# A list scheduler that lets the successive instructions of one engine overlap, and plans the exponential and the maximum of the softmax with other durations

## The chip, the core and the metric

The kernel runs on one core of a Trainium2 chip. The core has a matrix engine (TensorE, PE in the profile), a vector engine (VectorE, DVE), a scalar engine (ScalarE, ACT), a general engine (GpSimd, POOL) and a queue engine that here only issues DMAs (SyncE, SP). Each engine takes its own instructions strictly in the order in which the program lists them, and waits at semaphores for the others. The metric is the device time of one execution in microseconds, lower is better. Three executions of the kernel before took 2626.95, 2629.58 and 2632.05 us; the median is 2629.58 us.

## The reference

One block of a transformer over 2048 tokens of width 448: a layer norm, then attention with 16 heads of width 28 and a mixture of 8 experts, both added to the input. All 8 experts take part in every token (K = E = 8), so the mixture is dense and its gates are a plain softmax.

```python
xn = layernorm(x)
# attention, 16 heads of 28
q, k, v = split(xn @ wqkv)
p = softmax(q @ k.T * 28 ** -0.5)
out = x + (p @ v) @ wo
# mixture, for e in range(8):
out += gate[e] * (silu(xn @ w1[e]) @ w2[e])      # 448 -> 1792 -> 448
```

Inputs and output are float32.

## The kernel before

Every float32 factor of a large product is scaled by a power of two and split into two float16 halves, high and low, and the product is made of three float16 products. That multiplies PE's work, and it gives the other engines the work of splitting.

**Stages.** `phase0` loads and normalizes the input, makes queries, keys and values, writes them to DRAM, and prepares the first weights. Then two streams of work are mixed until the end.

- **The mixture** (`moe`): 24 groups of 4 or 5 blocks of 128 hidden columns. For each group the weights are loaded (`load_group`), their largest magnitudes are found and sent through DRAM so that all partitions have them (`group_scales`, `scales`: the DMA `mxs<-mxr` writes, the DMA `scmg<-mxs` reads, and DVE's chain from L358 to L368 makes the scale `scog` of it), and they are split on ACT (L463, L464, L481, L482) and POOL (L468, L485). The hidden products are L898 (with a small tail, L906), their activation goes ACT L940 (tanh), DVE L943, ACT L946 (high half) and POOL L947 (low half), the second products are L962, and DVE adds them up in L974.
- **Attention** (`attention`): 256 tiles, one for each head and 128 queries. A tile has two **scores** of 128 x 1024, each of two matmuls (L1058, 512 score pairs in all). DVE takes the row maximum of a score (L1062), ACT takes the exponential (L1076), ACT and DVE split the result (L1084 high, L1087 low), the halves are transposed by DMA (L1101), and PE multiplies them by the values (L1135, L1142). Only one score pair can be in PSUM at a time: it has banks 0 and 1, and the next pair waits until the exponential has read the last one. The six other banks hold all other products.

**What sets the order.** The program's order is not written by hand. Each piece of work is a `Job` with an engine, a planned duration `ns`, a due time `v` and its dependencies. `Plan.run` plays the plan through on a clock of its own: whenever an engine is free in the plan, it takes the ready job with the smallest due time whose buffers and banks are to be had, emits its instructions, and marks the engine busy for `ns`. What depends on the job becomes ready `ns` plus a lag later (180 ns behind PE, 60 ns behind ACT and DVE, 90 ns behind POOL). DMAs have a planned transfer time and a planned landing time. So planned durations decide the order on every engine, and on the chip nothing but this order is left of them.

```python
free[e] = t + j.ns
end = t + j.ns + j.lag
if j.size:
    dma = max(dma, t + 1000) + j.size
    end = dma + (LAND if j.v > 1 else 1000)
```

A maximum is planned at 1330 ns and an exponential at 1205 ns before the change.

Of the kernel before, what the change touches and what calls it, by code (L numbers as in the profile page):

```python
# [35 lines left out]
SEL = 512.0  # L36
NB, TL, TH = 4, 1, 4
RW1, RW2, RH, RP = 9, 9, 7, 1
QK_SCALE = DH ** -0.5
XS = 8.0  # L40
HUGE = 3.0e38
# [17 lines left out]
class Plan:  # L59
# [2 lines left out]


    LAG = {"PE": 180, "ACT": 60, "DVE": 60, "POOL": 90, "SP": 0}

    def __init__(self):
        self.jobs, self.wrote, self.read, self.order = [], {}, {}, {}
# [37 lines left out]
    def run(self, pools, banks):  # L105
# [3 lines left out]
        free = dict.fromkeys(self.LAG, 0)  # L109
        live, given = {}, {}  # L110
        events, t, dma, left = [], 0, 0, len(self.jobs)
# [42 lines left out]
        while left:  # L154
            moved = True
            while moved:
                moved = False
                for e in ready:
# [14 lines left out]
                        b.real = pools.get(b.pool).tile(b.shape, b.dtype, tag=b.tag, name=b.name, bufs=b.bufs)  # L173
                    j.fn()
                    left -= 1
                    free[e] = t + j.ns
                    end = t + j.ns + j.lag
                    if j.size:
                        dma = max(dma, t + 1000) + j.size
# [10 lines left out]
            t = events[0][0]  # L190
# [74 lines left out]
def block_kernel(ctx, tc, x, wqkv, wo, w_gate, w1, w2, out):  # L265
# [741 lines left out]
    def attention(at):  # L1007
# [39 lines left out]
        def score(i, j, v):  # L1047
            h, t = TILES[i]
            if i % NB == 0 and j == 0:
                mx[i] = buf("ap", [P, NB, 2], F32, f"mx{i}", tag="mx", bufs=3)  # L1050
            q0 = t % TPC * P
            sc[i, j] = b = ps_s(f"ps{i}_{j}")
            q, k, m, n = Q[h, t // TPC], K[h, j], mx[i // NB * NB], i % NB

            def product():
                for a in range(2):
                    cs = slice(a * C, (a + 1) * C)
                    nc.tensor.matmul(b()[:, cs], q()[:, q0 : q0 + P], k()[:, cs], start=True, stop=True)  # L1058

            add("PE", 2 * Z_NS, product, v, r=[(q, g) for g in range(4)] + [(k, g) for g in range(4)], w=[b])  # L1060
            def top():
                nc.vector.tensor_tensor_reduce(  # L1062
                    b(), b(), zero.to_broadcast([P, 2 * C]), cneg, HUGE,
                    op0=ALU.add, op1=ALU.min, accum_out=m()[:, n, j : j + 1],
                )

            add("DVE", 1330, top, v, r=["cexp"], w=[b, (m, n, j)])

        def expo(i, j, v):

            if j == 0:
                PR[i] = buf("ap", [P, S], F32, f"pf{i}", tag="pf", bufs=2)
            p, s, m, n = PR[i], sc.pop((i, j)), mx[i // NB * NB], i % NB

            def powers():
                nc.scalar.activation(p()[:, 2 * j * C : 2 * (j + 1) * C], s(), AF.Exp, bias=m()[:, n, j : j + 1], scale=-1.0)  # L1076

            add("ACT", 1205, powers, v, r=[s, (m, n, j)], w=[(p, j)])

        def halves(i, v):  # L1080
            p = PR.pop(i)
# [217 lines left out]
```

## Time and profile before

| | before |
|---|---|
| times of three runs, us | 2626.95, 2629.58, 2632.05 |
| the profiled execution's own time, us | 2628.33 |
| its span, first to last instruction, us | 2626.2 |
| PE busy, us (matmuls) | 2603.8 (17149) |
| DVE busy, us (instructions) | 2157.1 (3067) |
| ACT busy, us (instructions) | 1926.5 (2482) |
| POOL busy, us (instructions) | 1185.1 (1103) |
| granted TensorE clock | 1.000 |

The profile is of one execution. The span leaves out 2.1 us of the execution's time, which lie around the first and last instruction. Busy time is the time in which at least one instruction of the engine ran. In rows that group instructions, the number behind "x" is their count, then follow the busy time, the mean duration of one in ns, and the idle time of the engine just before them with what ended it. In rows of the timeline the first number is the start in us from the start of the span, the second the duration in us, and a bracket at the end gives the idle time before the row and who ended it. In rows of waits the engine and line that waited stand first, then who released it, the sum of the waits in us, their count and the longest.

### The profile page before, as it was taken

What the parts mean: (1) busy time and instruction counts of PE and PEld (TensorE: products, weight loads), DVE (VectorE), ACT (ScalarE), POOL (GpSimd) and SP (SyncE); (2) the same over time, 40 slices, a digit from 0 to 9 for tenths busy, and PEclk for the clock granted to TensorE, in tenths of its full rate; (3) what the DMA queues carried; (4) which work ended last, traced back from release to release, by engine and by line L of the source; (5) the groups of instructions that cost most, each with busy time, mean ns of one, the idle gap of its engine ahead of it and who ended that gap; (6) DMA issues with size and microseconds to landing.
All of it is one profiled execution on the core that took longest, in us unless ns stands there. A gap on an engine that the chain in (4) does not pass through costs nothing.

```text
span 2626.2 us, 45450 instructions
## 1 busy us (share of the span) xinstructions
PE 2603.8 (99%) x17149; PEld 1262.4 (48%) x17149; DVE 2157.1 (82%) x3067; ACT 1926.5 (73%) x2482; POOL 1185.1 (45%) x1103
## 2 busy tenths in 40 slices
PE   7999999999999999999999999999999999999999
PEld 3444444444444444444444444444444444444444
DVE  8578888888888888888888888978898779878875
ACT  5586887777877777777777778777777677776762
POOL 2243464436444444534534455454455334543533
PEclk9999999999999999999999999999999999999999
DMA  8657767667676777577675776666676667756663
GB/s 246 177 121 144 168 136 157 137 141 169 136 141 136 148 157 167 123 147 167 131 157 121 164 161 143 149 139 149 148 170 124 142 137 160 162 118 141 141 118 111
DMA packets 1207019, 387.52 MB, mean 148 GB/s; under 512 B 1142928, under 2 KB 1188368, under 8 KB 1206800
## 3 DMA queue, kind: packets, MB, share of 16 engines
q1 hardware_dynamic: 1206240, 384.61, 66.9%
q8 instruction: 134, 2.20, 0.4%
q14 instruction: 85, 0.70, 0.1%
q10 hardware_dynamic: 560, 0.02, 0.0%
HBM read 85.11 MB, written 15.23 MB: 38 GB/s over the span
## 4 chain that ended last, share of the span: by engine, by line
PE 94%; DVE 2%; DMA 1%; POOL 1%; ACT 1%; issue 1%; SPq 0%; DVEq 0%; POOLq 0%; ACTq 0%
PE banks L962 37%; PE banks L898 35%; PE banks L1058 8%; PE banks L1142 4%; PE banks L753 2%; PE banks L1135 2%; PE banks L906 2%; PE banks L776 1%; PE banks L1228 1%; DVE banks L1062 1%; DVE pl L1087 1%; DMA scmg<-mxs 0%; POOL hl L947 0%; ACT pf L1076 0%; ACT ph L1084 0%
## 5 line engine op out<-in xcount | busy, mean ns | idle before, releaser
L898 PE MATMUL banks<-xs,w 128*128 128x512 f16 x4480 | 1035.6, 379 | 1.0 <-DVE acc L974 0.9
L947 POOL TENSOR_TENSOR hl<-t,hh 128x512 f16<-128x512 f32 x448 | 607.9, 1369 | 850.3 <-ACT hh L946 772.2
L962 PE MATMUL banks<-w,hh 128*128 128x448 f16 x3584 | 970.8, 352 | 0.5 <-DVE t L943 0.5
L1076 ACT ACTIVATE pf<-banks,mx 128x1024 f32<-128x1024 f32 x512 | 569.3, 1112 | 368.8 <-DVE mx L1062 340.7
L1062 DVE CUSTOM_DVE_ANT_0 banks<-banks,zero,cneg 128x1024 f32<-128x1024 f32 x512 | 659.6, 1288 | 170.5 <-PE banks L1058 142.1
L898 PEld LDWEIGHTS <-w 128*128 128x128 f16 x4480 | 426.8, 97 | 547.1 <-issue 48.2
L962 PE MATMUL banks<-w,hl 128*128 128x448 f16 x1792 | 631.3, 352 | 0.0
L1087 DVE SCALAR_TENSOR_TENSOR pl<-pf,ph 128x2048 f16<-128x2048 f32 x256 | 611.1, 2387 | 3.9 <-DMA tl<-pl 1.8
L962 PEld LDWEIGHTS <-hh 128*128 128x128 f16 x3584 | 346.7, 98 | 350.9 <-issue 13.4
L1084 ACT ACTIVATE ph<-pf 128x2048 f16<-128x2048 f32 x256 | 487.8, 1905 | 32.2 <-DVE pl L1087 18.1
L940 ACT ACTIVATE t<-banks,the 128x512 f32<-128x512 f32 x448 | 295.9, 683 | 103.4 <-PE banks L898 35.1
L943 DVE SCALAR_TENSOR_TENSOR t<-t,banks 128x512 f32<-128x512 f32 x448 | 296.0, 681 | 63.6 <-ACT t L940 63.0
L974 DVE SCALAR_TENSOR_TENSOR acc<-banks,gwe,acc 128x448 f32<-128x448 f32 x384 | 257.1, 679 | 104.8 <-PE banks L962 103.0
L1058 PE MATMUL banks<-K,Q 112*128 112x512 f16 x1024 | 305.8, 379 | 2.3 <-ACT pf L1076 2.2
L946 ACT ACTIVATE hh<-t 128x512 f16<-128x512 f32 x448 | 267.5, 623 | 47.0 <-PE banks L962 35.5
L962 PEld LDWEIGHTS <-hl 128*128 128x128 f16 x1792 | 174.7, 98 | 164.3
L468 POOL TENSOR_TENSOR w<-r,w 128x512 f16<-128x512 f32 x112 | 156.0, 1400 | 140.4 <-ACT w L464 130.9
L485 POOL TENSOR_TENSOR w<-r,w 128x448 f16<-128x448 f32 x112 | 132.1, 1185 | 106.4 <-ACT w L482 103.2
L1058 PEld LDWEIGHTS <-Q 112*128 112x128 f16 x1024 | 95.2, 98 | 108.5 <-issue 17.0
L333 DVE TENSOR_REDUCE mx<-r 128x1 f32<-128x1280 f32 (+3 forms) x96 | 124.9, 1310 | 1.4 <-DMA r<-in_B_w_dram 1.4
L1142 PEld LDWEIGHTS <-th 128*128 128x128 f16 x4096 | 118.2, 96 | 13.7 <-issue 0.4
L1142 PE MATMUL banks<-V,th 128*128 128x57 f16 x4096 | 119.7, 188 | 0.0
(141 smaller groups left out, 1512.7 us busy)
## 6 DMA issues: line engine op xcount, KB each, us to landing
r<-in_B_w_dram SPq DMA_DIRECT2D x16, 1120.0 KB
r<-in_B_w_dram SPq DMA_DIRECT2D x16, 960.0 KB
K<-qk SPq DMA_DIRECT2D x128, 56.0 KB
Q<-qk SPq DMA_DIRECT2D x256, 28.0 KB
r<-in_B_w_dram SPq DMA_DIRECT2D x8, 896.0 KB
r<-in_B_w_dram SPq DMA_DIRECT2D x8, 768.0 KB
r<-in_B_w_dram SPq DMA_DIRECT2D x32, 160.0 KB
vs<-vt SPq DMA_DIRECT2D x4, 1024.0 KB
```

Source lines behind the costliest of these rows:

```text
L898: nc.tensor.matmul(z(), rows(w)[:, blk, :], xx, start=(i == 0 and not late), stop=(i == NTERM - 2 and late))
L940: add("ACT", 690, lambda: nc.scalar.activation(t(), z(), AF.Tanh, scale=th_()[:, 0:1]), v, r=[z, th_], w=[t])
L943: lambda: nc.vector.scalar_tensor_tensor(t(), t(), 1.0, z(), op0=ALU.add, op1=ALU.mult),
L946: add("ACT", 635, lambda: nc.scalar.activation(hh(), t(), AF.Copy), v, r=[t], w=[hh])
L947: add("POOL", 1425, lambda: nc.gpsimd.tensor_tensor(hl(), t(), hh(), ALU.subtract), v, r=[t, hh], w=[hl])
L962: nc.tensor.matmul(y()[:, 0:D], a, wv, start=(i == 0 and u == 0), stop=(i == g - 1 and u == 2))
L1058: nc.tensor.matmul(b()[:, cs], q()[:, q0 : q0 + P], k()[:, cs], start=True, stop=True)
L1062: nc.vector.tensor_tensor_reduce(b(), b(), zero.to_broadcast([P, 2 * C]), cneg, HUGE, op0=ALU.add, op1=ALU.min, accum_out=m()[:, n, j : j ...
L1076: nc.scalar.activation(p()[:, 2 * j * C : 2 * (j + 1) * C], s(), AF.Exp, bias=m()[:, n, j : j + 1], scale=-1.0)
L1084: add("ACT", 1910, lambda: nc.scalar.activation(h(), p(), AF.Copy, scale=P_SCALE), v, r=pk, w=[h])
L1087: lambda: nc.vector.scalar_tensor_tensor(l(), p(), P_SCALE, h(), op0=ALU.mult, op1=ALU.subtract), v,
L1142: nc.tensor.matmul(a()[:, n, kt // (NKT // 2), 0:n2], ths[n]()[:, kt], vb()[:, kt, 0:n2], start=(n == 0 and kt == 0), stop=(n == NB - 1 an ...
```

## The change

`Plan` gets a table `LEAVE`. A job on ACT, DVE or POOL gives its engine free 100, 80 or 40 ns before the job's planned end. The time at which its result is ready stays at the planned end plus the lag. The maximum is planned at 1350 ns in place of 1330, the exponential at 1120 in place of 1205. No instruction, buffer, bank, pool or due time is touched. Since two lines are added, the line numbers of the changed kernel are higher by one from L39 and by two from L65 on: L1062 becomes L1064, L1076 becomes L1078.

```diff
+OA, OD, OP = 100, 80, 40
...
     LAG = {"PE": 180, "ACT": 60, "DVE": 60, "POOL": 90, "SP": 0}
+    LEAVE = {"PE": 0, "ACT": OA, "DVE": OD, "POOL": OP, "SP": 0}
...
-                    free[e] = t + j.ns
+                    free[e] = t + j.ns - self.LEAVE[e]
                     end = t + j.ns + j.lag
...
-            add("DVE", 1330, top, v, r=["cexp"], w=[b, (m, n, j)])
+            add("DVE", 1350, top, v, r=["cexp"], w=[b, (m, n, j)])
...
-            add("ACT", 1205, powers, v, r=[s, (m, n, j)], w=[(p, j)])
+            add("ACT", 1120, powers, v, r=[s, (m, n, j)], w=[(p, j)])
```

The order changes on every engine, from the 64th row of PE on. Three places follow, with the rows of before first.

**ACT at the end of `phase0`**, where it copies the last queries and keys out of PSUM (`qh3_4` to `qh3_6`). Before, they stand alone, and the first activation of the mixture (`t0_0_0`) follows:

```order
L760 ACTIVATE qh3_4_1196<-banks_71 128x512
L760 ACTIVATE qh3_5_1214<-banks_71 128x512
L760 ACTIVATE qh3_6_1228<-banks_71 128x512
L940 ACTIVATE t0_0_0_1271<-banks_71,the0_928 128x512
L940 ACTIVATE t0_1_0_1276<-banks_71,the0_928 128x512
```

Now, on the same engine at the same place:

```order
L762 ACTIVATE qh3_4_1214<-banks_71 128x512
L465 ACTIVATE r1_1_955<-r1_1_955,scog1_1193 128x4x128
L466 ACTIVATE w1_1_0_1216<-r1_1_955 128x512
L465 ACTIVATE r1_1_955<-r1_1_955,scog1_1193 128x4x128
L466 ACTIVATE w1_1_1_1228<-r1_1_955 128x512
L762 ACTIVATE qh3_5_1243<-banks_71 128x512
L465 ACTIVATE r1_1_955<-r1_1_955,scog1_1193 128x4x128
L466 ACTIVATE w1_1_2_1246<-r1_1_955 128x512
L762 ACTIVATE qh3_6_1258<-banks_71 128x512
```

Three weight splits of group 1 (two rows each) have moved ahead of the last two copies; the first of them needs group 1's scale, `scog1`.

**DVE, the scale of group 1.** Before, the chain that makes `scog1` stands behind the second maximum of attention (L1062, two rows for each), and the third maximum follows it:

```order
L1062 ISA banks_71,mx0_1324<-banks_71,zero_79,cneg_87 128x1024
L1062 ISA mx0_1324 128x1
L358 TENSOR_REDUCE scbg1_1377<-scmg1_1346 128x2
L361 TENSOR_SCALAR scbg1_1377<-scbg1_1377 128x2
L362 TENSOR_SCALAR sceg1_1378<-scbg1_1377 128x2
L366 TENSOR_SCALAR scig1_1379<-sceg1_1378 128x1
L367 TENSOR_SCALAR scig1_1379<-sceg1_1378 128x1
L366 TENSOR_SCALAR scig1_1379<-sceg1_1378 128x1
L367 TENSOR_SCALAR scig1_1379<-sceg1_1378 128x1
L368 TENSOR_SCALAR scog1_1380<-scig1_1379 128x4
L943 SCALAR_TENSOR_TENSOR t0_4_0_1389<-t0_4_0_1389,banks_71 128x512
L1062 ISA banks_71,mx0_1324<-banks_71,zero_79,cneg_87 128x1024
```

Now the chain (L360 to L370 by the new line numbers) stands between the copies of the low halves of the last queries and keys, `ql3_3` and `ql3_4`:

```order
L764 TENSOR_TENSOR ql3_3_1187<-banks_71,qh3_3_1185 128x512
L360 TENSOR_REDUCE scbg1_1190<-scmg1_1166 128x2
L363 TENSOR_SCALAR scbg1_1190<-scbg1_1190 128x2
L364 TENSOR_SCALAR sceg1_1191<-scbg1_1190 128x2
L368 TENSOR_SCALAR scig1_1192<-sceg1_1191 128x1
L369 TENSOR_SCALAR scig1_1192<-sceg1_1191 128x1
L368 TENSOR_SCALAR scig1_1192<-sceg1_1191 128x1
L369 TENSOR_SCALAR scig1_1192<-sceg1_1191 128x1
L370 TENSOR_SCALAR scog1_1193<-scig1_1192 128x4
L439 TENSOR_SCALAR the1_1219<-scog1_1193 128x1
L440 TENSOR_TENSOR the1_1219<-the1_1219,scog1_1193 128x1
L764 TENSOR_TENSOR ql3_4_1223<-banks_71,qh3_4_1214 128x512
```

It has moved ahead of three copies, four activations and two maxima, and right behind the instruction that needs the DMA `scmg<-mxs` stands now `ql3_4`.

**DVE, the second and third maximum**, now, at the place of the first rows above:

```order
L1064 ISA banks_71,mx0_1371<-banks_71,zero_79,cneg_87 128x1024
L1064 ISA mx0_1371 128x1
L945 SCALAR_TENSOR_TENSOR t0_4_0_1426<-t0_4_0_1426,banks_71 128x512
L1064 ISA banks_71,mx0_1371<-banks_71,zero_79,cneg_87 128x1024
L1064 ISA mx0_1371 128x1
L945 SCALAR_TENSOR_TENSOR t0_0_1_1430<-t0_0_1_1430,banks_71 128x512
L1089 SCALAR_TENSOR_TENSOR pl0_1456<-pf0_1386,ph0_1438 128x2048
```

Between these two maxima one activation is left of the nine instructions before. On PE, 10 matmuls of L898 and 4 of L906 stand now between the two score pairs that they read, and 15 of L898 with the 4 of L906 before.

## The prediction

> **What bounds the kernel now.** The page comes first: busy times, then the chain of work that ended last.
>
> ```profile
> span 2626.2 us, 45450 instructions
> ...
> PE 2603.8 (99%) x17149; PEld 1262.4 (48%) x17149; DVE 2157.1 (82%) x3067; ACT 1926.5 (73%) x2482; POOL 1185.1 (45%) x1103
> ...
> PE 94%; DVE 2%; DMA 1%; POOL 1%; ACT 1%; issue 1%; SPq 0%; DVEq 0%; POOLq 0%; ACTq 0%
> ```
>
> PE is idle for 2626.2 - 2603.8 = 22.4 us, and the chain runs through PE. The other engines idle for 18% of the time or more. So the question is only where those 22.4 us lie. The view by windows says it:
>
> ```profile
> 0.00:100.00 100.00, 85.58 (x402) 41.68 (x403) 72.95 (x177) 51.46 (x101) 24.23 (x47) 1.00 0.78 217
> ...
> 2600.00:2700.00 100.00, 22.24 (x117) 11.16 (x115) 9.21 (x14) 2.90 (x5) 4.00 (x4) 0.99 0.06 21
> ```
>
> In the first 100 us PE (the first number behind the comma) lacks 14.4 us, and behind the last matmuls 26.2 - 22.2 = 4.0 us. For the 2500 us between, 22.4 - 14.4 - 4.0 = **4.0 us** are left. Who ended PE's waits:
>
> ```profile
> PE banks L371 <- DVE mav L333: 12.2, 1, 12.2
> PE banks L1058 <- ACT pf L1076: 2.2, 3, 1.2
> PE banks L776 <- ACT WA L567: 2.0, 1, 2.0
> PE banks L898 <- DVE acc L974: 0.9, 1, 0.9
> ```
>
> The waits of 12.2 and 2.0 us are the first weights, and the order starts to differ only behind them. So this is nearly all that a better order could win: 4.0 us, 0.15% of the time. A matmul's row is longer than the distance to the next one, so a wait shorter than that overhang doesn't show:
>
> ```profile
> L962 PE MATMUL banks<-w,hh 128*128 128x448 f16 x3584 | 970.8, 352 | 0.5 <-DVE t L943 0.5
> ...
> L962 PE MATMUL banks<-w,hl 128*128 128x448 f16 x1792 | 631.3, 352 | 0.0
> ```
>
> The row is 0.35 us, the distance 0.19 (below, under a). With some seven waits at 0.16 us each this hides about 1.1 us.
>
> **The change, part by part.** First, is the planned overlap real?
>
> ```profile
> 999.16 1.89 ACT L1084 ACTIVATE ph<-pf 128x2048 f16<-128x2048 f32 x1
> ...
> 999.96 1.48 DVE L333 TENSOR_REDUCE mx<-r 128x1 f32<-128x1280 f32 x1
> 1000.96 1.10 ACT L1076 ACTIVATE pf<-banks,mx 128x1024 f32<-128x1024 f32 x1
> ...
> 1001.35 2.28 DVE L1087 SCALAR_TENSOR_TENSOR pl<-pf,ph 128x2048 f16<-128x2048 f32 x1
> ```
>
> ACT's L1084 would end at 1001.05, and L1076 starts at 1000.96: 0.09 us of overlap, 0.10 in the table. On DVE, 999.96 + 1.48 = 1001.44 against 1001.35: 0.09, and 0.08 in the table. The plan comes closer to the chip. The Trainium skill has a rule against it, in "VectorE: DVE Perf Modes", section "The DRAIN you can't avoid": the next DVE instruction does not start until the pipe of the last one has emptied. By that rule the sum would be that of the last rival below, 2652; the rows disagree with it, and the measurement decides.
>
> The durations that change:
>
> ```profile
> L1062 DVE CUSTOM_DVE_ANT_0 banks<-banks,zero,cneg 128x1024 f32<-128x1024 f32 x512 | 659.6, 1288 | 170.5 <-PE banks L1058 142.1
> ...
> L1076 ACT ACTIVATE pf<-banks,mx 128x1024 f32<-128x1024 f32 x512 | 569.3, 1112 | 368.8 <-DVE mx L1062 340.7
> ```
>
> The plan has an exponential at 1120 where the chip has 1112, before at 1205. So the plan of before was slower than the chip on ACT and DVE, by about 0.1 us for each of some 5500 instructions. That error was harmless: PE's order was made for results that came later than they do, and each product found its input waiting. The change takes this margin away. It adds and removes no matmul, so PE's work stays, and what can move is idle time: down by 4.0 us (5.1 with the hidden part), or up. The terms:
>
> **(a) Score pairs that stand too close.** How near two pairs can follow:
>
> ```profile
> 260.31 0.60 PE L1058 MATMUL banks<-K,Q 112*128 112x512 f16 x2
> ...
> 261.05 1.29 DVE L1062 CUSTOM_DVE_ANT_0 banks<-banks,zero,cneg 128x1024 f32<-128x1024 f32 x1 [0.99 <-PE banks L1058]
> ...
> 262.44 1.12 ACT L1076 ACTIVATE pf<-banks,mx 128x1024 f32<-128x1024 f32 x1 [0.99 <-DVE rl L1178]
> ...
> 263.61 0.59 PE L1058 MATMUL banks<-K,Q 112*128 112x512 f16 x2
> ```
>
> The next pair starts 0.05 us behind the exponential's end (262.44 + 1.12 = 263.56), and the cycle is 3.30 us. PE's work between two pairs follows from the order by the paces in the chain:
>
> ```profile
> 2455.93 4.54 PE banks L962 x24
> ...
> 2592.53 4.32 PE banks L898 x20
> ```
>
> 0.189 us for an L962, 0.216 for an L898 or a score. Added up, 11 pairs stood less than 3.3 us behind the last one, all at 3.27. Now it is 31, 15 at 3.27 and 16 at 3.19 to 3.24 (one is the third pair, shown with the change). At worst the 20 new ones cost 16 x 0.09 + 4 x 0.03 = 1.6 us; where the maximum starts quicker behind its matmuls they cost nothing. I take the middle, **0.8 us**.
>
> **(b) Delays that the plan doesn't know.** How such a delay reaches PE:
>
> ```profile
> 2291.66 0.42 DVE L358 TENSOR_REDUCE scbg<-scmg 128x2 f32<-128x256 f32 x1 [2.06 <-DMA scmg<-mxs]
> 2292.11 1.15 DVE L361 TENSOR_SCALAR scbg<-scbg 128x2 f32<-128x2 f32 x1
> ...
> 2293.99 1.29 DVE L1062 CUSTOM_DVE_ANT_0 banks<-banks,zero,cneg 128x1024 f32<-128x1024 f32 x1
> ...
> 2296.54 0.59 PE L1058 MATMUL banks<-K,Q 112*128 112x512 f16 x2 [1.20 <-ACT pf L1076]
> ```
>
> DVE stood 2.06 us before L358, whose DMA was late, L361 took 1.15 us for two numbers in each lane, the maximum behind them came late, and PE waited 1.20 us. DVE's wait for that DMA over the whole run:
>
> ```profile
> DVE scbg L358 <- DMA scmg<-mxs: 6.9, 6, 2.3
> ```
>
> 6 of 24 exchanges. The delays stay with the new order; what changes is the slack in which they vanish. Pairs less than 4.0 us apart rise from 75 to 141 of 511, those less than 4.5 us from 245 to 266, so a delay of 0.7 us finds twice as many open places and one of 1.2 us hardly more. I let the 4.0 us of now grow by 40%: **+1.6 us**. Bounds: -4.0 if all vanish, and +25 if each of the 24 exchanges costs 1.20 (28.8 less the 4.0).
>
> **(c) The scale of group 1 at the end of `phase0`.** ACT now splits group 1's weights ahead of the last copies out of PSUM, and what hangs on those copies has no slack:
>
> ```profile
> 79.83 0.39 SPq L312 DMA_DIRECT2D mxs<-mxr  x1
> ...
> 82.83 0.60 ACT L760 ACTIVATE qh<-banks 128x512 f16<-128x512 f32 x1 [1.64 <-PE banks L753]
> ...
> 89.47 0.42 DVE L358 TENSOR_REDUCE scbg<-scmg 128x2 f32<-128x256 f32 x1 [0.58 <-DMA scmg<-mxs]
> ...
> 90.91 0.72 ACT L463 ACTIVATE r<-r,scog 128x512 f32<-128x512 f32 x1 [0.32 <-DVE scog L368]
> ...
> 92.20 0.71 ACT L463 ACTIVATE r<-r,scog 128x512 f32<-128x512 f32 x1
> ...
> 122.20 0.38 SPq L312 DMA_DIRECT2D mxs<-mxr  x1
> ...
> 122.80 0.60 ACT L760 ACTIVATE qh<-banks 128x512 f16<-128x512 f32 x1 [1.89 <-PE banks L753]
> ...
> 128.31 1.67 SPq L312 DMA_DIRECT2D Q<-qk  x4
> ...
> 131.87 0.60 PE L1058 MATMUL banks<-K,Q 112*128 112x512 f16 x2
> ```
>
> The last copy starts at 122.80, its stores follow, then SP issues the loads of K and Q, the last of Q at 128.31 + 1.67 = 129.98, and PE's first score runs at 131.87, 1.9 us later. I read that as just in time: whatever delays the last copy delays the first score, and nothing covers it, since PE's order is fixed. When does the scale come? Group 0's exchange took 89.47 - 79.83 = 9.6 us, and its first split started 1.4 us later; a shorter exchange took 7.5 us:
>
> ```profile
> 1514.78 0.36 SPq L312 DMA_DIRECT2D mxs<-mxr  x1
> ...
> 1522.25 0.41 DVE L358 TENSOR_REDUCE scbg<-scmg 128x2 f32<-128x256 f32 x1
> ```
>
> Group 0's first split, at 90.91 so far, now stands ahead of the copy that ran at 82.83, so it comes about 8 us earlier; group 1's loads wait for group 0's splits, and its four row maxima stand closer together. So I place its `mxs<-mxr` 8 to 12 us before 122.20, at 110 to 114, and the scale at 110 + 7.5 + 1.4 = 119 to 114 + 9.6 + 1.4 = 125. Three splits at 92.20 - 90.91 = 1.3 us and a copy of some 0.5 stand between the scale and the last copy, 4.4 us; without delay it would need the scale by 118.4. The delay is 0.6 to 6.6 us. I take **2.0 us**, in the lower half, because group 1's loads, which shared the DMA engines with all that ran between 100 and 118 us, have landed by then; bounds 0 and 6.6.
>
> The rest I cost at nothing. Attention's last score moves some 30 us forward and the mixture ends alone, but PE's last matmuls are the same second products, and the 4.0 us behind them stay. POOL has 55% idle time to hide its new order.
>
> **Sum:** 0.8 + 1.6 + 2.0 = 4.4 us. On the profiled execution's 2628.33 us this gives 2632.7. That execution lies 1.25 us under the median of three, 2629.58; on it the sum is **2634.0**, 0.17% slower. A measurement of this kernel tells about 0.2% from no change, 5.3 us.
>
> **The rivals.**
>
> *The waits vanish.* A plan nearer to the chip puts each product where its input is ready, and the 4.0 us of waits go with the hidden 1.1: 2629.6 - 5.1 = 2624.5, and under 2624.3 with a little luck. For it: the overlap is real. Against it: the waits there are come from late DMAs and stretched small steps, which the new plan knows no better.
>
> *No net effect.* The new order meets as many waits as the old one, (a) and (c) are hidden: 2629.6. That the order doesn't change is excluded by its rows.
>
> *Slower: DVE held at an exchange.* One mechanism: the chain from L358 stands in DVE's queue when the plan thinks that the data has landed, the DMA is later, and the copies or maxima behind it are late for PE. An idler DVE in the plan puts the chain nearer to the planned landing. For it: the 2.06 us and the 1.20 us above, exchanges of 7.5 to 9.6 us, (c). Against it: 18 of 24 exchanges find the data landed now. Price: (c) in the middle of its bounds, 3.3, and 1.2 us for each further exchange that hits; with four of them 0.8 + 3.3 + 4.8 = 8.9, 2638.5; with eight, 2643.3. With the forecast's (a) and (b) it decides from 2.9 us in (c) on, or with one further exchange that hits.
>
> *The overlap isn't there on DVE.* Then two DVE jobs between two near score pairs are planned 0.08 us too short each, and the 141 pairs under 4.0 us lose up to 0.16 us: 22.6 us, 2652. Against it stand the two rows above, where DVE starts 0.09 us before the last end.
>
> **Chances.** The forecast, a loss under 0.2%: 0.44. No net effect: 0.10. The waits vanish: 0.06, half of it over 0.2%. Slower, DVE held: 0.39. No overlap: 0.01. So faster 0.03, same 0.57, slower 0.40. The range goes from 2625, where most of the waits vanish, to 2647, eight exchanges that hit and (c) at its upper bound; it leaves out the far end of (b), +25 us. The forecast's own range is 2631 to 2635.
>
> **What would show it.** (a): PE's waits for ACT L1078 (the new L1076), in many small pieces at 3.2 us. (b): more idle time of DVE before L360 for `scmg<-mxs`, and PE's idle time in the middle over 4.0 us. (c): PE idle before the first score, near 132 us, and the window from 100 to 200 us below 100. The forecast is wrong if PE's idle time in the middle stays at 4 us or falls (the margin was not needed), or if it grows past 10 us (the margin carried the kernel); and (c) is wrong if the first score runs at 132.

## The result, and the profile after

The changed kernel takes **2667.62 us** (median of 4 runs, 2665.72 to 2670.28) beside 2630.82 for the one before (4 runs): a ratio of 1.0141, 95% interval 1.0128 to 1.0154, 36.8 us slower. The forecast was 2634.0 with a range up to 2647. The profiled execution of the changed kernel took 2670.28 us. In its line numbers the score is L1060 and the long product `pl` L1089.

The page of the changed kernel:

```profile
span 2668.3 us, 45461 instructions
...
PE 2617.3 (98%) x17149; PEld 1263.3 (47%) x17149; DVE 2164.8 (81%) x3067; ACT 1921.2 (72%) x2482; POOL 1213.2 (45%) x1103
...
PE 70%; DVE 12%; ACT 7%; issue 4%; DMA 4%; POOL 2%; SPq 0%; ACTq 0%; DVEq 0%; POOLq 0%
```

The span grew by 42.1 us. PE's idle time went from 22.4 to 51.0 us, and its busy time rose by 13.5 with the same 17149 matmuls. That can only be waits that are hidden because a matmul's record overhangs the next one, and slower matmuls; both are shown below. PE holds 70% of the chain; it held 94%. The view by windows of the changed kernel says where PE idles (the granted clock is the third number from the end):

```profile
0.00:100.00 100.00, 82.52 (x386) 40.02 (x387) 72.82 (x176) 54.92 (x108) 29.80 (x51) 1.00 0.78 220
100.00:200.00 100.00, 97.46 (x535) 45.24 (x534) 66.12 (x106) 64.43 (x89) 30.51 (x30) 0.98 0.53 133
200.00:2600.00 2400.00, 2372.68 (x15906) 1147.28 (x15905) 2004.13 (x2752) 1786.57 (x2262) 1137.18 (x1007) 1.00 0.68 145
2600.00:2700.00 100.00, 64.61 (x328) 30.76 (x326) 21.73 (x34) 15.26 (x25) 15.72 (x16) 1.00 0.11 40
```

and of the kernel before, for the middle:

```profile
200.00:2600.00 2400.00, 2395.95 (x16081) 1163.17 (x16080) 2005.52 (x2768) 1799.79 (x2276) 1119.89 (x1018) 1.00 0.68 145
```

In the first 200 us PE idles 17.5 + 2.5 = 20.0 us (14.4 before), from 200 to 2600 us 27.3 (4.0 before), behind the last matmuls 68.3 - 64.6 = 3.7 (4.0 before). Most of the loss is spread over the middle. Who ended the waits:

```profile
PE banks L1060 <- ACT pf L1078: 18.3, 32, 1.2
...
DVE scbg L360 <- DMA scmg<-mxs: 16.7, 12, 3.5
...
PE banks L755 <- DVE ql L764: 4.6, 3, 2.5
...
PE banks L755 <- DVE the L439: 1.8, 1, 1.8
```

The wait of a score for the exponential of the pair ahead of it went from 2.2 us in 3 pieces to 18.3 in 32. The record of the matmul ahead overhangs the next start by 0.16 us (0.35 us long at a distance of 0.19 for a second product, 0.38 at 0.22 for a score), so each piece hides 0.16 more: 23.4 against 2.7 us, **20.7 us of the loss**. Waits too short to outlast the overhang are not in it.

How a score comes to wait, in the timeline of the changed kernel:

```profile
575.97 1.08 DVE L335 TENSOR_REDUCE mx<-r 128x1 f32<-128x896 f32 x1
...
576.97 0.68 DVE L945 SCALAR_TENSOR_TENSOR t<-t,banks 128x512 f32<-128x512 f32 x1
...
577.57 2.29 DVE L1089 SCALAR_TENSOR_TENSOR pl<-pf,ph 128x2048 f16<-128x2048 f32 x1
577.76 0.60 PE L1060 MATMUL banks<-K,Q 112*128 112x512 f16 x2
579.77 1.29 DVE L1064 CUSTOM_DVE_ANT_0 banks<-banks,zero,cneg 128x1024 f32<-128x1024 f32 x1
...
581.49 1.11 ACT L1078 ACTIVATE pf<-banks,mx 128x1024 f32<-128x1024 f32 x1
...
582.64 0.59 PE L1060 MATMUL banks<-K,Q 112*128 112x512 f16 x2 [0.37 <-ACT pf L1078]
```

The pair's matmuls end at 578.36, but DVE runs without a gap through a row maximum, a product and the long product, and gets to the pair's maximum at 579.77, 1.4 us late. The exponential ends at 582.60, and the next pair starts 0.04 us behind it. The maximum stands in DVE's queue. This is not one case. Counted over the whole trace, 90 of the 512 maxima start more than 1 us behind the end of their pair's matmuls, 39 before, and DVE is never idle ahead of one of the 90; 52 of them stand right behind a long product. 22 of the 32 waits above follow such a maximum. In the waits of DVE the same is seen from the other side, before and after: DVE comes to a maximum ahead of its score, and waits for it, in 128 cases where there were 190.

```profile
DVE banks L1062 <- PE banks L1058: 142.1, 190, 3.2
```

```profile
DVE banks L1064 <- PE banks L1060: 113.2, 128, 2.9
```

The plan knows nothing of these waits. Played through on the clock of `Plan.run`, the changed order has no wait of PE ahead of a score, and it ends 3.0 us earlier than the order of before.

The second place is phase 0, here at group 1's exchange, first DVE, then PE, of the changed kernel:

```profile
119.37 0.69 DVE L764 TENSOR_TENSOR ql<-banks,qh 128x512 f16<-128x512 f32 x1 [1.68 <-ACT qh L762]
123.53 0.42 DVE L360 TENSOR_REDUCE scbg<-scmg 128x2 f32<-128x256 f32 x1 [3.46 <-DMA scmg<-mxs]
...
125.22 0.69 DVE L764 TENSOR_TENSOR ql<-banks,qh 128x512 f16<-128x512 f32 x1
```

```profile
118.76 4.70 PE L755 MATMUL banks<-xs,WA 128*128 128x512 f16 x21
125.97 3.98 PE L755 MATMUL banks<-xs,WA 128*128 128x512 f16 x11 [2.51 <-DVE ql L764]
```

DVE stood 3.46 us for the exchange's data, the copy `ql` behind it in the queue frees a PSUM bank, and PE waited 2.51 us for that bank. Then 11 matmuls took 3.98 us, 0.36 each, where 21 just ahead took 0.22 each; that is another 1.5 us. Three more waits of L755 stand ahead of it. One, 1.76 us at 85.65 us, comes behind group 0's exchange, for whose data DVE stood 2.85 us. The other two, 0.51 us at 38.92 and 1.59 us at 43.05, have no exchange ahead of them: there DVE is busy without a gap, and `ql` stands behind other work. The first score shows the sum, since the same matmuls stand ahead of it in both orders:

```profile
139.30 0.60 PE L1060 MATMUL banks<-K,Q 112*128 112x512 f16 x2
```

It ran at 131.87 before: phase 0 costs **7.4 us**. With the 20.7 that makes 28.1 of the 42.1 us by which the span grew. The rest is found in the distances between the starts of matmuls, set against the usual distance of the same two products before: ahead of scores they grew by some 24 us in all, so 4 us are waits too short for a record to show, and ahead of other products by some 10 us, over half of that at L1230.

### The profile page after: what moved, and what is told of

It is laid out like the page before. It is cut to its first block, busy times and chain, and to the rows that moved or that the text cites. A ratio compares the mean times of both kernels' runs of the same rounds, so it can differ in the third digit from the quotient of the medians.

```text
span 2668.3 us, 45461 instructions
## 1 busy us (share of the span) xinstructions
PE 2617.3 (98%) x17149; PEld 1263.3 (47%) x17149; DVE 2164.8 (81%) x3067; ACT 1921.2 (72%) x2482; POOL 1213.2 (45%) x1103
## 4 chain that ended last, share of the span: by engine, by line
PE 70%; DVE 12%; ACT 7%; issue 4%; DMA 4%; POOL 2%; SPq 0%; ACTq 0%; DVEq 0%; POOLq 0%
PE banks L964 28%; PE banks L900 25%; PE banks L1060 6%; PE banks L1144 4%; DVE banks L1064 3%; DVE pl L1089 3%; ACT pf L1078 2%; ACT ph L1086 2%; PE banks L1137 2%; PE banks L908 2%; DMA scmg<-mxs 1%; POOL hl L949 1%; DVE t L945 1%; PE banks L1230 1%; PE banks L755 1%
## 5 line engine op out<-in xcount | busy, mean ns | idle before, releaser
L949 POOL TENSOR_TENSOR hl<-t,hh 128x512 f16<-128x512 f32 x448 | 629.2, 1419 | 863.8 <-ACT hh L948 788.5
L1078 ACT ACTIVATE pf<-banks,mx 128x1024 f32<-128x1024 f32 x512 | 569.0, 1111 | 365.6 <-DVE mx L1064 336.1
L1064 DVE CUSTOM_DVE_ANT_0 banks<-banks,zero,cneg 128x1024 f32<-128x1024 f32 x512 | 658.4, 1286 | 134.1 <-PE banks L1060 113.2
L1089 DVE SCALAR_TENSOR_TENSOR pl<-pf,ph 128x2048 f16<-128x2048 f32 x256 | 625.4, 2443 | 13.3 <-ACT ph L1086 7.3
L1060 PE MATMUL banks<-K,Q 112*128 112x512 f16 x1024 | 305.5, 379 | 19.1 <-ACT pf L1078 18.3
L470 POOL TENSOR_TENSOR w<-r,w 128x512 f16<-128x512 f32 x112 | 157.2, 1410 | 137.0 <-ACT w L466 130.3
L487 POOL TENSOR_TENSOR w<-r,w 128x448 f16<-128x448 f32 x112 | 136.7, 1231 | 81.9 <-ACT w L484 80.7
L1060 PEld LDWEIGHTS <-Q 112*128 112x128 f16 x1024 | 95.1, 98 | 135.3 <-issue 50.0
L1168 POOL TENSOR_TENSOR ls<-tt 128x232 f32<-128x232 f16 x64 | 48.5, 757 | 207.5 <-DMA tt<-lt 207.4
```

Of the source, the lines that this page charges most:

```text
L949: add("POOL", 1425, lambda: nc.gpsimd.tensor_tensor(hl(), t(), hh(), ALU.subtract), v, r=[t, hh], w=[hl])
L1064: nc.vector.tensor_tensor_reduce(b(), b(), zero.to_broadcast([P, 2 * C]), cneg, HUGE, op0=ALU.add, op1=ALU.min, accum_out=m()[:, n, j : j ...
L1089: lambda: nc.vector.scalar_tensor_tensor(l(), p(), P_SCALE, h(), op0=ALU.mult, op1=ALU.subtract), v,
```

## The experiments

All are the changed kernel with the edit shown; the diffs are against it. Times are medians of 3 to 11 executions, of 2 for one that is named. Each was compared with the kernel before on the same chip (its median lay between 2630.3 and 2631.3).

**The two halves of the change.**

```diff
-            add("DVE", 1350, top, v, ...
+            add("DVE", 1330, top, v, ...
-            add("ACT", 1120, powers, v, ...
+            add("ACT", 1205, powers, v, ...
```

> The overlap alone (100, 80 and 40 ns), with the planned durations of before (maximum 1330, exponential 1205 ns). Theory M (the margin): a plan that counts every ACT, DVE and POOL job longer than it is leaves unplanned gaps on these engines, in which a late step catches up; without them the maximum and the exponential stand in a queue. Then the overlap brings most of the loss of 36.8 us: 2652 to 2668, with many small PE waits ahead of scores. Theory N (near pairs): what costs is the pairs that stand closer than a score, a maximum and an exponential take. By the order, 10 pairs stand less than 3.3 us apart here (11 before, 31 with the whole change), so the waits for the exponential go back to about those of before, and the time to 2631 to 2642 (phase 0 may still lose up to 9). Theory X (exchanges): the loss comes from steps that wait on the small DMAs between two partitions' views, whose landing is planned too early in all versions: 2645 to 2668, with DVE's wait for scmg at 12 us or more.

```diff
-OA, OD, OP = 100, 80, 40
+OA, OD, OP = 0, 0, 0
```

> The durations alone (maximum 1350, exponential 1120 ns), no overlap. Theory M: most of the margin is still there (only 0.085 us of each of 512 exponentials is gone, 0.02 us is added for each maximum): 2628 to 2638. Theory N: 19 pairs less than 3.3 us apart against 11 and 31, so about 40% of the score waits, 10 us: 2638 to 2646. Theory X: 2628 to 2640, depending on how the exchanges fall.

The overlap alone: 2644.75 us, ratio 1.0058 (1.0041 to 1.0074). The durations alone: **2627.05 us**, 0.9987 (0.9977 to 0.9996), a little faster than before. The times do not add: +14, -4, and +37 together. The durations cost nothing: N's 2638 to 2646 for them is excluded, though that order has 19 pairs under 3.3 us (11 before), and M's 2628 and X's 2628 are just missed. The overlap alone costs 14 us, and no theory had that: M said 2652 or more and N 2642 at most, and X's range began at 2645, 0.25 above (its sign, 12 us or more of DVE's waits for `scmg`, came with 12.5). What remains of M is that the loss needs the overlap. In the waits of the durations alone the score hardly shows, and DVE finds the exchanges better than before:

```profile
DVE scbg L360 <- DMA scmg<-mxs: 3.9, 7, 1.0
...
PE banks L1060 <- ACT pf L1078: 0.6, 2, 0.4
```

**Results planned later, engines as tight as in the change.**

```diff
-    LAG = {"PE": 180, "ACT": 60, "DVE": 60, "POOL": 90, "SP": 0}
+    LAG = {"PE": 180, "ACT": 160, "DVE": 140, "POOL": 130, "SP": 0}
```

> The whole change, but results are planned later by what the overlap takes off: ACT's 60 to 160 ns, DVE's 60 to 140, POOL's 90 to 130. An engine may take its next job as early as in the change, but what hangs on a result is planned as late as the overlap-less plan had it. By the order no pair is left under 3.3 us, 95 under 4.0 (141 with the change, 75 before). Theory N: the near pairs are gone, so the score waits fall back to about 3 us: 2635 to 2648 (phase 0 may stay). Theory M: what is missing is room on the engines, which this does not give back, and the chain of two steps gains 0.18 us of slack only: 2648 to 2664. Theory X: no help, 2655 to 2670.

2645.47 us, 1.0055 (1.0040 to 1.0070): in N's range and 2.5 us under M's, and the waits of scores for the exponential are down to 4.2 us in 7 pieces, near N's 3. Since N failed on the durations alone, this doesn't bring it back; it says that late results give back more than M thought.

**All loads planned to land later.**

```diff
-M_AT, A_AT, LEAD, END, LAND = 60.0, 0.0, 130.0, 2585.0, 2000
+M_AT, A_AT, LEAD, END, LAND = 60.0, 0.0, 130.0, 2585.0, 3500
-                        end = dma + (LAND if j.v > 1 else 1000)
+                        end = dma + (LAND if j.v > 1 else 2500)
```

> The whole change, with every DMA planned to land 1.5 us later (3.5 for 2.0 us, in phase 0 2.5 for 1.0). 53 pairs stand less than 3.3 us apart (31 with the change). Theory X: DVE's wait for scmg falls from 16.7 us to under 6, the four waits of PE in phase 0 (7 us, with the slow matmuls behind them 9) go, and the waits ahead of scores with them: 2632 to 2648. Theory M: only phase 0 gains, the score waits stay near 24 us: 2655 to 2664. Theory N: with more near pairs the score waits grow: 2662 to 2680.

2796.34 us, 1.0632 (1.0616 to 1.0648): a miss of every theory. In the windows of this run the stage up to 2600 us is better than in the change (PE idles 12.4 us from 200 to 2600), and the end is ruined:

```profile
200.00:2600.00 2400.00, 2387.56 (x15690) 1154.19 (x15689) 1932.28 (x2658) 1718.19 (x2207) 1139.07 (x994) 1.00 0.63 136
2600.00:2794.00 194.00, 71.78 (x514) 31.02 (x513) 101.61 (x130) 77.34 (x75) 19.38 (x32) 0.57 0.57 132
```

With loads planned later attention falls behind the mixture and is left alone at the end, where the scores wait for exponentials 102.8 of the run's 110.9 us. The edit was too coarse for its question; the run with only the exchanges put off asks it again.

**One slack given back at a time.** First the exponential's result, then DVE's overlap, then ACT's and POOL's.

```diff
-            add("ACT", 1120, powers, v, r=[s, (m, n, j)], w=[(p, j)])
+            add("ACT", 1120, powers, v, r=[s, (m, n, j)], w=[(p, j)]).lag += 100
```

> The whole change, but the exponential's result alone is planned 100 ns later (what waits for it may start 160 ns behind its planned end, not 60); how long it holds ACT stays as in the change. The first four runs gave +14 us for the overlap alone, -4 for the durations alone, +37 for both. Theory J (just in time): the overlap sets the engines' queues tight, and it is the exponential's result, planned 85 ns sooner, that puts PE's next score where no late maximum is forgiven. Then this edit gives back what the planned duration of 1205 gave: 2640 to 2650, with less than 10 us of PE waits ahead of scores. Theory Q (the queue on ACT): the 85 ns matter because ACT's own queue is planned too full; then nothing comes back here, 2658 to 2670. Theory S (scatter): each order falls anywhere in a band of some 40 us; then any time from 2630 to 2670, and no order among the edits.

```diff
-OA, OD, OP = 100, 80, 40
+OA, OD, OP = 100, 0, 40
```

> The whole change without the overlap on DVE (ACT 100, POOL 40 kept). Theory D: the maxima that come late stand behind a packed DVE queue, since the plan with 80 ns of overlap counts DVE's long product (2395 less 80 = 2315 ns) shorter than it is; with the 80 ns back, the score waits fall from some 27 to under 10 us and phase 0's stay: 2632 to 2648. Theory J: the exponential's result is as early as in the change and 30 pairs stand under 3.3 us (31), so half of the loss stays at least: 2648 to 2662. Theory S: no prediction.

```diff
-OA, OD, OP = 100, 80, 40
+OA, OD, OP = 0, 80, 0
```

> The whole change with the overlap on DVE alone (ACT and POOL 0). Theory D: nearly all of the loss, 2652 to 2668. Theory J: the exponential's result is early and DVE's queue tight, so also most of it: 2650 to 2665. Theory Q: ACT's queue has its room back, 2632 to 2645. The runs with and without DVE's overlap are to be read against each other: under D and J together this one is clearly the slower of the two, under Q the faster.

2641.92 us (1.0045, 1.0028 to 1.0062), 2648.42 (1.0063, 1.0048 to 1.0078) and 2645.89 (1.0057, 1.0042 to 1.0072). The first is in J's range, and so is the second, by 0.4 us. The third is in none: Q ends at 2645 and J begins at 2650. With DVE's overlap alone and without it the times are alike, where D and J wanted one clearly slower and Q the other. So none of the three theories holds; the pieces take off 26, 19 and 22 of 37 us.

**Only the exchanges planned later**, by 0.5 us for `mxs` and 2.0 us for `scmg`.

```diff
-            dma(lambda: mxs[group], lambda: mx(), v, r=[mx], w=[("mxs", group)], kb=1)
+            dma(lambda: mxs[group], lambda: mx(), v, r=[mx], w=[("mxs", group)], kb=1).lag = 500
...
-                r=[("mxs", group)], w=[pb], kb=128,
-            )
+                r=[("mxs", group)], w=[pb], kb=128,
+            ).lag = 2000
...
-                        end = dma + (LAND if j.v > 1 else 1000)
+                        end = dma + (LAND if j.v > 1 else 1000) + (j.lag if j.lag >= 500 else 0)
```

> The whole change, with only the two DMAs of each exchange (mxs and scmg) planned later, by 0.5 and 2.0 us; all other loads as before. Later landing of all loads had brought phase 0 back but put off attention. Theory X: DVE's 16.7 us before L360 fall under 4, phase 0's four PE waits and the slow matmuls behind them (9 us) go, and of the score waits those that come from a held DVE, 3 to 8 us: 2648 to 2658. Theory Y: the exchanges are a part of phase 0 only, 2656 to 2662. Theory S: no prediction.

2655.61 us, 1.0091 (1.0075 to 1.0108), 12.0 us under the change: in theory X's range, and only 0.4 us under Y's, so the time does not part the two. Its waits, its window from 100 to 200 us, and its first score:

```profile
PE banks L1060 <- ACT pf L1078: 15.5, 28, 2.1
...
DVE scbg L360 <- DMA scmg<-mxs: 0.9, 1, 0.9
```

```profile
100.00:200.00 100.00, 99.75 (x553) 46.23 (x552) 71.82 (x114) 70.30 (x96) 34.81 (x32) 1.00 0.54 136
```

```profile
132.27 0.60 PE L1060 MATMUL banks<-K,Q 112*128 112x512 f16 x2
```

L360 waits for an exchange once, for 0.9 us, and PE's 2.5 us of idle time in that window are 0.25. The first score stands at 132.27 where it stood at 139.30, though five more matmuls are ahead of it; the two early waits of phase 0 without an exchange are still there (0.51 and 1.60 us). The waits ahead of scores are hardly less (15.5 for 18.3). So the exchanges were the main cause in phase 0, and not in the middle. (The edit also makes another order, so 12.0 is not theirs to the last microsecond; see below.)

**How much overlap.** Half of it; the long product planned as long as it runs; a gap in its place; and the two edits that had helped together.

```diff
-OA, OD, OP = 100, 80, 40
+OA, OD, OP = 50, 40, 20
```

> The whole change with half of the overlap (50, 40, 20 ns). Runs so far: overlap 0 gives 2627, full 2668, full on one side (DVE, or ACT and POOL) 2646 to 2648. Theory M (each job's spare time in the plan is a margin, and the loss grows the faster the less of it is left): between, and nearer to no overlap, 2634 to 2648. Theory S (scatter, any order of this kind falls anywhere between 2630 and 2670): no prediction, a time above 2655 or under 2630 would speak for it.

```diff
-                "DVE", 2395,
+                "DVE", 2480,
```

> The whole change, with DVE's long product (pl) planned at 2480 for 2395 ns, so that with 80 ns of overlap it holds DVE for 2400 in the plan; before it held it 2395. It is the one large group that the change plans shorter than it runs. Theory P: the packed DVE queue comes from this one group; with it back, the loss goes as with no overlap on DVE at all, 2642 to 2652. Theory M: the margin of all jobs counts, this is 256 of some 3000 on DVE (a quarter of its busy time, and 85 of some 80 x 3000 / 256 = 940 ns that the overlap takes between two of them): 2656 to 2666.

```diff
-OA, OD, OP = 100, 80, 40
+OA, OD, OP = -50, -40, -20
```

> The new durations, and a planned gap behind each job in place of the overlap (ACT 50, DVE 40, POOL 20 ns). Theory M: more margin; what is left to win over no overlap (2627) is the few us of waits in the middle, and attention's last score moves later, 2584 by PE's work (2592 with no overlap, 2536 with the change): 2624 to 2630. Theory S: no prediction.

Overlap 0, and the exchanges later as above:

> The new durations, no overlap, and the two DMAs of an exchange planned 0.5 and 2.0 us later: the two edits that helped, together. Theory X: DVE's wait before L360 goes (3.9 us with the durations alone), and half of PE's few waits in the middle with it: 2623 to 2628, faster than before by 0.1 to 0.3%. If the exchanges cost nothing where there is margin: 2626 to 2630.

2639.05 us for half (1.0036, 1.0023 to 1.0049), as M said; 2649.18 for the longer `pl` (1.0070, 1.0057 to 1.0084), in P's range and below M's, though two orders further down reach the same time without it; 2629.46 for the gap (0.9994, 0.9985 to 1.0003), as M said; 2633.91 for the exchanges without overlap (1.0014, 1.0005 to 1.0023), a miss: the two edits do not help together. The waits of the run with the gap:

```profile
DVE scbg L360 <- DMA scmg<-mxs: 11.5, 10, 3.5
...
PE banks L1060 <- ACT pf L1078: 0.9, 2, 0.8
```

Of the 11.5 us, 7.9 in nine waits lie behind 200 us, and there PE hardly feels them: 0.9 us ahead of scores. The tenth, 3.5 us in phase 0, does reach PE, and the first score stands at 135.27:

```profile
99.30 8.63 PE L778 MATMUL banks<-WA,xs 128*128 128x456 f16 x44 [1.89 <-DVE ql L764]
```

So in the middle, where the queues have reserve, late exchanges cost next to nothing, and there planning for them has little to win. Why the exchanges planned later were even 7 us slower than the durations alone is not shown; three waits of scores (2.8 us) are a part.

**Other orders with the same margin.** Each single edit took off 12 to 26 us. Either the pieces work together, or the change's own order is a bad draw.

```diff
-OA, OD, OP = 100, 80, 40
+OA, OD, OP = 97, 78, 39
```

> The whole change with overlaps of 97, 78 and 39 for 100, 80 and 40 ns: as good as the same margin, another order. Theory M (the margin sets the loss): 2658 to 2672. Theory S (the whole change's 2668 is a bad draw, and full and partial versions scatter about 2648): 2640 to 2656.

```diff
-OA, OD, OP = 100, 80, 40
+OA, OD, OP = 103, 82, 41
```

> The same with 103, 82 and 41 ns. Theory M: 2660 to 2675. Theory S: 2640 to 2656.

```diff
-M_AT, A_AT, LEAD, END, LAND = 60.0, 0.0, 130.0, 2585.0, 2000
+M_AT, A_AT, LEAD, END, LAND = 62.0, 0.0, 130.0, 2585.0, 2000
```

> The whole change, with the mixture's due times starting at 62 for 60: the same planned durations and overlaps, another order. Theory M: 2658 to 2672. Theory S: 2640 to 2656.

The same due times with the overlap at 0:

> The durations alone (no overlap), with the mixture's due times starting at 62 for 60. With the margin there, both theories expect a narrow spread: 2625 to 2634; a time over 2640 would show that orders with margin scatter as widely as those without.

2647.79 (1.0062, 1.0039 to 1.0085), 2645.82 (1.0057, 1.0033 to 1.0081), 2658.82 (1.0106, 1.0069 to 1.0143; two executions), and without overlap **2625.39** (0.9979, 0.9968 to 0.9990). Both theories are half right. Four orders with the change's margin give 2646, 2648, 2659 and 2668, mean 2655.0: they spread over 22 us, and the change's is the worst of them. Three with the new durations and no overlap, or a gap, give 2625.4, 2627.1 and 2629.5, mean 2627.3. The two groups lie 16 us apart at their nearest (12 if the two orders with exchanges planned later, 2633.91 and 2655.61, are counted in), and half of the overlap, 2639.05, lies between. So the overlap costs 27.7 us on the mean of these orders, and 12.6 us more are this one's draw. Single comparisons of one piece with 2668 prove little. The waits follow the times; half of the overlap, then 103%, then the other due times:

```profile
DVE scbg L360 <- DMA scmg<-mxs: 7.5, 7, 1.8
...
PE banks L1060 <- ACT pf L1078: 4.8, 12, 0.9
```

```profile
DVE scbg L360 <- DMA scmg<-mxs: 10.3, 8, 3.6
...
PE banks L1060 <- ACT pf L1078: 6.5, 19, 0.7
```

```profile
DVE scbg L360 <- DMA scmg<-mxs: 17.1, 13, 2.8
...
PE banks L1060 <- ACT pf L1078: 14.2, 21, 1.9
```

Under 1 us without overlap (0.6 and 0.9 above; 2.8 with the exchanges planned later), then 4.8, 6.5, 14.2 and 18.3: the score's wait for the exponential orders the times 2639, 2646, 2659 and 2668. The late maxima go with them: 26 to 56 in the four orders without overlap, 58 with half, 61, 69 and 90. Near pairs do not: the order without overlap that gave 2633.91 has 30 of them under 3.3 us, by the prediction's paces, as many as the change.

**Which margin: late results or room on the engines.** Results later by twice as much; and once, under the other due times.

```diff
-    LAG = {"PE": 180, "ACT": 60, "DVE": 60, "POOL": 90, "SP": 0}
+    LAG = {"PE": 180, "ACT": 260, "DVE": 220, "POOL": 170, "SP": 0}
```

> The whole change, with results planned later by twice what the overlap takes off (ACT 260 for 60, DVE 220 for 60, POOL 170 for 90); the engines are still planned as tight as in the change. Four orders with the change's margin gave 2646, 2648, 2659 and 2668, so a single comparison with 2668 settles little, and this one goes by the four and by the once-later version (2645.5). Theory L (a late result in the plan is as good a margin as an idle engine): back to the orders with margin, 2624 to 2632. Theory O (what is missing is room on the engines, in which a late job catches up): 2638 to 2650.

```diff
-    LAG = {"PE": 180, "ACT": 60, "DVE": 60, "POOL": 90, "SP": 0}
+    LAG = {"PE": 180, "ACT": 160, "DVE": 140, "POOL": 130, "SP": 0}
...
-M_AT, A_AT, LEAD, END, LAND = 60.0, 0.0, 130.0, 2585.0, 2000
+M_AT, A_AT, LEAD, END, LAND = 62.0, 0.0, 130.0, 2585.0, 2000
```

> Results later by what the overlap takes off, as in the run that gave 2645.5, with the mixture's due times from 62 for 60; to be read against 2658.8, the change with those due times. If the later results help by themselves: 2634 to 2646, as with the first due times. If 2645.5 was a lucky draw among orders of the change's kind: 2648 to 2665.

2643.60 (1.0051, 1.0036 to 1.0066) and 2635.96 (1.0021, 1.0012 to 1.0031). The doubled one is in theory O's range and not in L's; the other is where later results that help would put it. Later results help by themselves: 22.1 us with the first due times (2667.62 less 2645.47) and 22.9 with the second (2658.82 less 2635.96). But all three versions, 2636.0 to 2645.5, stay above every kernel without overlap, 2625.4 to 2633.9, and twice as much wins 1.9 us further. What the doubled version still loses:

```profile
DVE scbg L360 <- DMA scmg<-mxs: 11.8, 7, 4.4
...
PE banks L1060 <- ACT pf L1078: 3.7, 9, 0.8
...
PE banks L755 <- DVE the L439: 3.1, 1, 3.1
```

```profile
100.00:200.00 100.00, 96.78 (x531) 44.86 (x530) 62.89 (x102) 62.08 (x86) 30.13 (x27) 0.98 0.52 127
```

```profile
140.18 0.60 PE L1060 MATMUL banks<-K,Q 112*128 112x512 f16 x2
```

The scores wait little, and 50 maxima are late. Much of what is left is phase 0: an exchange reaches PE in one wait of 3.1 us (L439), and the first score stands at 140.18, 8.3 us later than before (1.1 of them five more matmuls ahead of it), and the whole version is 13.0 us slower. With the other due times it is 4.1 us late, in a version 5.4 us slower. So late results take nearly all of the loss out of the waits ahead of scores, and much less of it out of phase 0. The times alone therefore say more against theory L than these traces do.

## Why the prediction was wrong, step by step

*What bounds it, and the direction*: right. PE's work stayed, only idle time moved, and the forecast was a loss. The text named its own falsifier, idle time in the middle past 10 us, "the margin carried the kernel": between the first 100 us and the tail it is now 51.0 - 17.5 - 3.7 = 29.8 us.

*Is the overlap real*: right. The rival without overlap on DVE gave 2652, but its mechanism isn't what happened: in the timeline above DVE's 577.57 product starts 0.08 us before the one ahead of it ends (576.97 + 0.68 = 577.65). The rule of the Trainium skill that the text sets against this, in "VectorE: DVE Perf Modes", section "The DRAIN you can't avoid", goes on to say that a next instruction that is not held starts earlier. So page and rows need not disagree. The plan came nearer to the chip, and the kernel slower.

**(b), the delays that the plan doesn't know: the step that failed.** It was taken at +1.6 us with bounds of -4 and +25; the waits ahead of scores alone grew by at least 20.7. The range to 2647 had left the far end of (b) out; even with it, and with (a) and (c) at their bounds, 2629.6 + 25 + 1.6 + 6.6 = 2662.8 stays under the measured time. The failing sentence is "The delays stay with the new order; what changes is the slack in which they vanish". Neither half of it held. DVE's waits at exchanges went from 6.9 to 16.7 us, and the slack that counts was not the distance of two pairs but the reserve on DVE: 90 maxima came late out of its queue where there were 39. The sum scaled 4.0 us by the number of near pairs, as if that number said how often a delay meets PE. The runs that move the overlap alone show the size: none 2625 to 2627, a gap 2629, half 2639, full 2646 to 2668. That the nearness of pairs is not the measure, the orders without overlap show: with 19, 23 and 30 pairs under 3.3 us they are 4 and 6 us faster and 4 us slower than before. That a late step was caught up thanks to the reserve, and now isn't, is the reading that fits these runs; no run follows one late step through both orders. The late maxima don't come in long chains: 58 of the 90 have a punctual one on either side.

*(a), near pairs*: taken at 0.8, bound 1.6 us. The many small pieces came, 32 of them, but not for this reason, as shown under (b).

*(c), the scale of group 1*: the source was right, the path and the size were not. It was taken at 2.0 us (0 to 6.6). The text placed the scale at 119 to 125 us and took the lower half; it was ready at 124.9, and the text's own 118.4 would have made that 6.5 us. The exchange held DVE, and PE felt it at its PSUM banks at 125.97 us, through the copy `ql` in DVE's queue, not through ACT's splits and the loads of K and Q. That stall cost 2.5 us, the slow matmuls behind it 1.5. Three other waits of L755, 3.9 us, one of them at group 0's exchange, were not foreseen; with them the first score is 7.4 us late. The stated test, that the first score moves from 132, came out as said.

*The rival "DVE held at an exchange"* (2638 to 2643) had this part: 12 waits of DVE for `scmg` where there were 6. It was read as the whole of the bad case and is its smaller part: with the exchanges planned later 24.4 of 36.8 us of loss remain.

*"That error was harmless"*, said of the long planned durations, was half right. As long as nothing overlaps in the plan the exponential's 1205 for 1112 ns was harmless, as the run with the durations alone shows; with the overlap, going back to it took off 23 us (2644.75 against 2667.62), about as much as orders with the same margin differ by. The missing overlap was not harmless but useful.

What stays open: which of the pieces of margin counts most. The kernels with one piece given back lie between 2636 and 2656, within or under the spread of orders without any (2646 to 2668), and only the later results were tried on two orders. POOL's 40 ns were never taken off alone, though some of its groups run longer than the change plans them: L487 takes 1231 ns on the mean, where 1140 - 40 = 1100 are planned. Why one order falls 20 us behind another with a margin 3% apart was not settled either; more late maxima go with it, but what makes more of them late in one order than in another was not found.

A version that beats both kernels is the new durations without overlap: 2625.39 us with the due times at 62, 0.21% under the kernel before (interval 0.10 to 0.32%), and 2627.05 with the old ones. A third order of that kind, with the exchanges planned later, was 0.14% slower than before, so this gain is itself within what the order decides.

## What to carry to other kernels

A plan whose jobs are longer than on the chip holds a reserve for all that it doesn't know; before its durations are corrected, put that reserve somewhere on purpose, and price the correction by what queues behind a late step, not by the pairs that stand near. Where a number sets an order, time three or four neighbours of it: here 3 ns of overlap on ACT, 2 on DVE and 1 on POOL moved the kernel by 20 us, more than most single edits were thought to tell. And where an edit takes reserve away, a wait that cost next to nothing with it (7.9 us of DVE at exchanges in the middle, in the run with the gap) is to be counted as a possible cost.

## What the runs showed of the hardware that was not expected

*PE's granted clock falls behind a short stop.* The wait of 2.51 us at 125.97 us was enough, as the windows of the changed kernel show:

```profile
118.00:126.00 8.00, 5.49 (x27) 2.38 (x25) 2.96 (x13) 2.16 (x4) 0.00 (x0) 1.00 0.51 107
126.00:130.00 4.00, 4.00 (x12) 1.51 (x12) 0.75 (x2) 3.38 (x7) 2.81 (x3) 0.61 0.27 90
```

The clock goes from 1.00 to 0.61 on the mean of 4 us, and a wait of 2.5 us costs 4. The same happens at 1273.56 us behind a wait of 2.22 us (0.57 over 4 us). Behind the 1.76 us wait in the row below the matmuls ran at 2.53 / 11 = 0.23 us, the usual pace:

```profile
85.65 2.53 PE L755 MATMUL banks<-xs,WA 128*128 128x512 f16 x11 [1.76 <-DVE the L439]
```

The Trainium skill, "TensorE: Matmul & The Clock Gate", section "HAM oscillation — how this bites in real kernels", speaks of idle gaps over about 3.4 us; here 2.51 us sufficed. No length of wait from which the clock falls comes out of these runs: without overlap and with the exchanges planned later, a wait of 2.38 us at 2208.55 leaves it at 1.00.

*A step of eight numbers in each lane can take as long as the longest product.* All 64 of them in the changed kernel (shortest, median, longest in ns), then the longest, and POOL's rows at that time:

```profile
L1127 DVE TENSOR_TENSOR c<-top,mx x64: 166/168/2842, 173.1 to 2579.2; 128x8 f32<-128x8 f32 x64
```

```profile
2457.48 2.84 DVE L1127 TENSOR_TENSOR c<-top,mx 128x8 f32<-128x8 f32 x1
```

```profile
2456.91 3.39 POOL L949 TENSOR_TENSOR hl<-t,hh 128x512 f16<-128x512 f32 x3
```

The step ends at 2460.32, POOL's three products at 2460.30. It is no single case. 21 of the 64 steps take over 0.25 us, and each of them ends 0.02 to 0.03 us behind the end of a product of POOL (L949, L470 or L487); of those that ran while POOL stood idle none was long, though five ran short beside a product. So POOL's product holds the step, as far as rows can show it, for up to 2.7 us that no planned duration knows. The kernel before has 21 such steps too, so they are not what the change made worse.
